# Attention and a maxout layer on one core: fewer turning products, idle products in the opening, bounds of the weights by other products

## The chip, the core and the metric

The kernel runs on one core of a Trainium2 chip. The time is the device time of one execution in microseconds (us), from launch to end, as the median of several runs. The profile is one further execution recorded by the hardware profiler; its span runs from the first to the last instruction of the core.

## What is computed

Queries and keys are normalised per row, an ordinary softmax attention over 448 positions follows for 8 batches of 12 heads, and the heads' outputs, side by side, are the rows of a layer that takes the largest of three products and multiplies it by a fourth matrix:

```python
q, k, v: (8, 12, 448, 64); g_q, g_k: (64,); w1, w2, w3, w_out: (768, 768)

def rmsnorm(x, g):
    rms = np.sqrt(np.mean(x * x, axis=-1, keepdims=True) + 1e-06)
    return x / rms * g
q_n, k_n = (rmsnorm(q, g_q), rmsnorm(k, g_k))
scores = (1.0 / np.sqrt(64)) * np.matmul(q_n, k_n.transpose(0, 1, 3, 2))
scores = scores - np.max(scores, axis=-1, keepdims=True)
attn = np.exp(scores)
attn = attn / (np.sum(attn, axis=-1, keepdims=True) + 1e-09)
attn_out = np.matmul(attn, v)

x = attn_out.transpose(0, 2, 1, 3).reshape(8 * 448, 768)
h = np.maximum(np.maximum(x @ w1, x @ w2), x @ w3)
return h @ w_out
```

Queries, keys, values and gains come as 32-bit floats; the four weight matrices come as 64-bit floats, which the chip loads as pairs of 32-bit words (`raw` tiles) and decodes to 32-bit floats.

## The kernel before

**Groups and beats.** Two heads of a batch make a group `g` (48 of them, six to a batch). The program is one hand-written order: `for g: for i in range(12): beat(g, i)`. A beat puts work on the five engines' queues, and each engine takes its own queue strictly in that order. `later(n, work)` puts work off by `n` beats; `tick()` at a beat's end emits what is due. `thirds(n)` puts about `n` pieces of the maxout layer (three matmuls each) behind the attention's work of a beat, from a queue of batches; a batch of the layer is queued when its six groups are through, so the layer begins with group 6, and after the last group what is left of it runs alone.

**Plain groups.** The first six groups (`g < PLAIN`) work in 32-bit floats throughout: `turn_whole` turns a group's normalised rows (7 blocks of 128 rows by 64) by products with an identity on TensorE, `keep_whole` copies them to SBUF on ScalarE, `scores` multiplies, `row_max` (VectorE) takes the largest of each row, `softmax` (ScalarE) writes `e`, `turn_plain` and `keep_turned` turn it, `add_values` multiplies by v, and `spread_sums` and `keep_sums` spread the reciprocals of the row sums over the 64 columns of each head. From group 6 on, each operand is split in two 16-bit parts, three products stand for one, and turning is done by DMA; those groups are not touched here.

**Opening.** Ahead of the first beat, groups 0 and 1 are loaded, squared (`squares`), summed (`sum_squares`), their inverse root mean squares are taken with a power on GpSimd (`inv_rms`), and group 0 is scaled and turned. `prep_gain` works out the gain's scale with some small operations on VectorE and a power on GpSimd.

**Weights.** 24 blocks of 128 x 768 (18 of w1, w2, w3, in six threes, then 6 of w_out) are loaded, rebased on ScalarE, decoded in three steps on VectorE (`prep_block`), and split in 16-bit parts by `upper` (ScalarE) and `lower` (VectorE), one block every 4 beats and then every 8. The split needs a scale. `bound_in`, once for three blocks, bounds their columns by 18 products of the blocks' upper halves with themselves, into one PSUM tile of 128 x 128, takes each row's largest (`row_largest`), and `largest` takes the largest over partitions: a product that turns the column, a reduction on one partition, and a product that spreads the number over 128 partitions. `clear` sends it to GpSimd for a square root, and `scale` on VectorE copies, inverts and scales it. For w_out each block's largest entry comes from a reduction over its 768 columns in SBUF, and `bound_out` combines them, again with `largest`.

**PSUM.** One pool of three banks (`tag="m"`) serves turned rows, turned weights, bounds and the layer's accumulators `acc`; a bank is given again when it was read.

## Time and profile before

| | |
|---|---|
| median of 3 runs | 1035.94 us |
| the three runs | 1033.67, 1035.94, 1036.47 us |
| profiled execution, its own time | 1033.57 us |
| its span | 1031.8 us |
| mean granted TensorE clock | 0.985 |
| TensorE matmul busy | 988.9 us (96%) |
| VectorE busy | 697.5 us (68%) |
| ScalarE busy | 622.8 us (60%) |
| GpSimd busy | 598.5 us (58%) |

PE is TensorE's matmuls, PEld its weight loads, DVE VectorE, ACT ScalarE, POOL GpSimd, SP the engine whose queue issues most DMAs; SPq and ACTq are the queues' own instructions. `L841` is line 841 of the kernel. A row of a group of instructions names the tile written, `<-`, and the tiles read; in brackets stands how long the engine was idle before, and what ended that. A matmul of 32-bit floats shows as two matmul records. A row of stretches gives, for each engine, its busy time and its number of instructions, then the granted clock of TensorE and the mean share of the DMA engines. In the first 24 us the clock column shows 1.00, though the same products take about twice as long there as later; there their durations tell the clock. As matmuls are pipelined and their ends modelled, a duration of several matmuls holds some 0.2 us of latency.

### The profile page before, as it was taken

To read this page: it belongs to the slowest core of one execution; us is meant where nothing else is said; L and a number is where in the kernel's file an instruction comes from. 1 tells how busy PE (TensorE), PEld (TensorE's weight loads), DVE (VectorE), ACT (ScalarE), POOL (GpSimd) and SP (SyncE) were. 2 spreads that over 40 slices of the span, in tenths; PEclk is the share of its full clock that TensorE was granted. 3 is DMA by queue.
4 is the path that set the end of the run, shared out by engine and by line. 5 is a ranking of instruction groups with operands and counts; after the bars stand their busy time and mean duration, and the time that the engine had idled before them with its cause. 6 is when DMAs were issued, how large, how long until landed. Compare 5 with 4: busy or idle time off the path is not lost.

```text
span 1031.8 us, 17413 instructions
## 1 busy us (share of the span) xinstructions
PE 988.9 (96%) x5988; PEld 530.6 (51%) x5988; DVE 697.5 (68%) x1343; ACT 622.8 (60%) x1419; POOL 598.5 (58%) x652
## 2 busy tenths in 40 slices
PE   5999789898899999999999999999999999999998
PEld 3655444444455555555555555555555555555555
DVE  4898989987676856776667767786777666760120
ACT  3787866667666676666665666666665766651111
POOL 5566676765766666756666576676675766410000
PEclk9999879999999999999999999999999999999999
DMA  8866698997999999999999899999999998861001
GB/s 200 202 178 172 165 204 164 177 166 134 209 173 171 167 182 210 168 172 151 221 171 188 152 216 181 177 169 180 193 168 169 179 201 145 135 104 59 1 1 62
DMA packets 524089, 165.99 MB, mean 161 GB/s; under 512 B 500321, under 2 KB 519777, under 8 KB 524001
## 3 DMA queue, kind: packets, MB, share of 16 engines
q1 hardware_dynamic: 460992, 148.89, 74.8%
q10 hardware_dynamic: 63008, 16.00, 8.7%
q8 instruction: 47, 0.77, 0.3%
q14 instruction: 42, 0.34, 0.1%
HBM read 53.35 MB, written 11.01 MB: 62 GB/s over the span
## 4 chain that ended last, share of the span: by engine, by line
PE 74%; DVE 2%; ACT 1%; DMA 1%; issue 1%; SPq 0%; ACTq 0%
PE acc L841 41%; PE acc L903 15%; PE av L812 8%; PE sc L633 8%; PE sc L640 1%; DVE pp L767 1%; DVE nm L655 1%; DMA pt<-pp 1%; ACT sc L671 0%; DVE w_sb L335 0%; DVE ss L413 0%; DMA out_dram<-osb 0%; SPq L786 0%; ACT w_sb L330 0%; ACT pp L757 0%
## 5 line engine op out<-in xcount | busy, mean ns | idle before, releaser
L841 PE MATMUL acc<-xt,w_sb 128*128 128x448 f16 x2592 | 516.8, 355 | 0.0
L841 PEld LDWEIGHTS <-w_sb 128*128 128x128 f16 x2592 | 252.5, 98 | 245.0 <-issue 16.8
L671 ACT ACTIVATE sc<-sc,nm 128x448 f32<-128x448 f32 x294 | 178.8, 608 | 197.0 <-DVE nm L655 192.5
L655 DVE TENSOR_REDUCE nm<-sc 128x2 f32<-128x896 f32 x192 | 186.3, 970 | 101.5 <-PE sc L640 51.4
L757 ACT ACTIVATE pp<-sc,rs 128x448 f16<-128x448 f32 x294 | 172.8, 633 | 77.9 <-issue 29.2
L767 DVE SCALAR_TENSOR_TENSOR pp<-sc,rs,pp 128x448 f16<-128x448 f32 x294 | 188.0, 675 | 3.3 <-ACT pp L757 3.2
L427 POOL TENSOR_TENSOR ri<-ri,half_neg 128x7 f32<-128x7 f32 x96 | 148.8, 1550 | 8.0
L903 PE MATMUL acc<-w_sb,ht 128*128 128x384 f16 x864 | 148.6, 327 | 0.0
L461 POOL TENSOR_TENSOR kp<-kn,kp 128x448 f16<-128x448 f32 x42 | 44.7, 1065 | 167.6 <-ACT kp L455 154.5
L633 PE MATMUL sc<-kt,qt 128*128 128x448 f16 x504 | 117.6, 356 | 10.4 <-DVE pp L767 7.7
L903 PEld LDWEIGHTS <-ht 128*128 128x128 f16 x864 | 83.8, 99 | 60.2 <-issue 5.8
L633 PEld LDWEIGHTS <-qt 128*128 128x128 f16 x504 | 48.8, 98 | 56.0 <-issue 6.9
L812 PE MATMUL av<-pt,vp 128*64 128x448 f16 x672 | 72.2, 355 | 0.7 <-DMA pt<-pp 0.6
L870 POOL COPY hx<-ht 128x128 f16<-128x128 f16 x48 | 15.3, 318 | 94.3 <-DVE ht L865 94.3
L413 DVE TENSOR_REDUCE ss<-sq 128x7 f32<-128x448 f32 x96 | 57.6, 601 | 11.4 <-ACT sq L404 8.3
L595 POOL TENSOR_TENSOR vp<-vr,vp 128x512 f16<-128x512 f32 x42 | 50.0, 1189 | 22.6 <-ACT vp L589 22.6
L750 DVE TENSOR_SCALAR rs<-sc 128x2 f32<-128x2 f32 (+1 forms) x168 | 26.2, 156 | 50.4 <-ACT sc L671 50.3
L827 DVE SCALAR_TENSOR_TENSOR xt<-av,xt 128x448 f16<-128x448 f32 x42 | 26.2, 623 | 49.0 <-ACT xt L826 49.0
L461 POOL TENSOR_TENSOR qp<-qn,qp 128x448 f16<-128x448 f32 x42 | 46.2, 1100 | 19.2 <-ACT qp L455 16.9
L855 DVE TENSOR_TENSOR m<-acc,m 128x448 f32<-128x448 f32 x48 | 29.6, 617 | 37.7 <-PE acc L841 37.5
L812 PEld LDWEIGHTS <-vp 128*64 128x64 f16 x672 | 35.0, 109 | 35.0 <-issue 15.5
L861 ACT ACTIVATE ht<-acc 128x448 f16<-128x448 f32 x48 | 26.2, 546 | 41.8 <-DVE acc L855 41.8
(130 smaller groups left out, 1181.4 us busy)
## 6 DMA issues: line engine op xcount, KB each, us to landing
raw<-in_moe_w_dram SPq DMA_DIRECT2D x18, 768.0 KB, 4.5
kt<-kt SPq DMA_DIRECT2D x84, 112.0 KB, 2.5
out_dram<-osb SPq DMA_DIRECT2D x24, 384.0 KB, 3.7
vr<-in_v_dram SPq DMA_DIRECT2D x42, 192.0 KB, 4.1
kr<-in_k_dram ACTq DMA_DIRECT2D x34, 224.0 KB, 3.3
qr<-in_q_dram ACTq DMA_DIRECT2D x34, 224.0 KB, 4.6
raw<-in_moe_w_out_dram SPq DMA_DIRECT2D x6, 768.0 KB, 5.0
vs<-vp SPq DMA_DIRECT2D x84, 48.0 KB, 2.1
```

What stands on the lines that cost most here:

```text
L413: nc.vector.tensor_reduce(sums[g % 2][:, KQ[what]], sq, axis=AX, op=ALU.add)
L427: nc.gpsimd.tensor_tensor(out=ri, in0=ri, in1=half_neg[:, at], op=ALU.pow)
L461: nc.gpsimd.tensor_tensor(out=parts[:, :, 1], in0=n, in1=parts[:, :, 0], op=ALU.subtract)
L595: nc.gpsimd.tensor_tensor(out=vp[:, 1], in0=values_of(g).rearrange("p h n d -> p (h n) d"), in1=vp[:, 0], op=ALU.subtract,)
L633: nc.tensor.matmul(sc[:, h, :S], qt[:, 4 * h + c], kt[:, n, keys[h]], start=n == 0, stop=n == 1,)
L655: nc.vector.tensor_reduce(nm[:, :n], sc[:, :n, :S], axis=AX, op=ALU.max, negate=True)
L671: nc.scalar.activation(to, sc[:, h, :S], AF.Exp, bias=nm[:, h:h + 1], accum_out=total,)
L757: nc.scalar.activation(pp[:, h, 0], sc[:, h, :S], AF.Copy, scale=rs[:, h:h + 1])
L767: nc.vector.scalar_tensor_tensor(out=pp[:, h, 1], in0=sc[:, h, :S], scalar=rs[:, h:h + 1], in1=pp[:, h, 0], op0=ALU.mult, op1=ALU.subtract,)
L812: nc.tensor.matmul(av[half, :S], values, pt[:, 7 * h + block, SHIFT[h]:SHIFT[h] + S], start=n == 0, stop=n == len(steps) - 1,)
L841: nc.tensor.matmul(acc[:, :S], wt[:, wp, c], xs[c][:, xp], start=(c == 0 and n == 0), stop=(c == NCT - 1 and n == 2),)
L903: nc.tensor.matmul(acc[:, :HW], lhs, wo_sb[:, f, wp, half * HW:(half + 1) * HW], start=(f == 0 and n == 0), stop=(f == NFT - 1 and n == 2),)
```

## The change

Nothing of groups 6 to 47 or of the maxout layer changes. In short:

1. 36 products of the identity with itself, as 16-bit numbers, stand first on TensorE's queue; nothing reads their tile `idle`.
2. `turn_whole` turns the seventh block by two products of 64 x 64 (one to each half) in place of three wider ones; to match, the order of head 1's rows is rotated, q and k tiles hold 448 columns in place of 512, the keys are written in four interleaved runs by `keep_whole`, and v's first batch is loaded in runs of four rows (three DMAs in place of four).
3. q and k of a plain group are loaded by two DMAs in place of three; group 0's use both SP's and ACT's queue.
4. The opening is reordered: both groups are squared first, group 1's sums stand ahead of group 0's scaling on VectorE, and `prep_gain` comes last.
5. `spread_sums` alternates between the halves.
6. `largest` is gone: one product with a matrix of ones adds the rows' largest over partitions. `clear` comes two beats sooner, GpSimd raises to the power -0.5 and scales with a second instruction, `scale` has no VectorE operation of its own, and the split of three blocks begins three beats sooner.
7. Each block of w_out is bounded by 6 products of its upper halves and a reduction of 128 columns, in place of a reduction of 768; `bound_out` takes the roots on GpSimd.

```diff
+WARM = 36
...
+    idle = ps_m.tile([P, 512], F32, name="idle", tag="m")
+    bits = ident.bitcast(BF16)
+    for _ in range(WARM):
+        nc.tensor.matmul(idle[:, :2 * P], bits[:, :P], bits, start=True, stop=True)
...
         if kind == "out":
-            later(5, lambda: row_largest(o_row[:, ft:ft + 1], f), True)
+            bound_block(ft, f)
...
+        def products():
+            box.append(ps_m.tile([P, 512], F32, name="marks", tag="m"))
+            halves = f.bitcast(BF16).rearrange("p (n t) -> p n t", t=2)
+            for c in range(NCT):
+                part = halves[:, c * P:(c + 1) * P, 1]
+                nc.tensor.matmul(
+                    box[0][:, 0:P], part, part, start=c == 0, stop=c == NCT - 1
+                )
+
+        later(6, products)
+        later(8, lambda: row_largest(o_row[:, ft:ft + 1], box[0][:, 0:P]), True)
...
         def reduce():
             row_largest(most, box[0][:, 0:P])
-            largest(most, clear, (1, 1, 2, 1))
...
+        def spread():
+            box.append(ps_m.tile([P, 512], F32, name="most", tag="m"))
+            nc.tensor.matmul(
+                box[1][:, 0:1], ones_c.broadcast_to([P, P]), most, start=True, stop=True
+            )
...
-            nc.gpsimd.tensor_tensor(out=w_up[:, ft:ft + 1], in0=most, in1=root, op=ALU.pow)
-            later(2, scale)
+            up = w_up[:, ft:ft + 1]
+            nc.gpsimd.tensor_tensor(out=up, in0=most, in1=half_neg[:, 0:1], op=ALU.pow)
+            nc.gpsimd.tensor_scalar(
+                out=up, in0=up, scalar1=2.0 * UP, scalar2=1.0, op0=ALU.mult, op1=ALU.mult
+            )
+            later(3, scale)
 
         def scale():
-            top, up = w_most[:, ft:ft + 1], w_up[:, ft:ft + 1]
-            nc.vector.tensor_copy(top, up)
-            nc.vector.reciprocal(up, top)
-            nc.vector.tensor_scalar(
-                out=up, in0=up, scalar1=2.0 * UP, scalar2=None, op0=ALU.mult
-            )
+            up = w_up[:, ft:ft + 1]
...
-                later(2 + 4 * j, lambda n=n, f=f: upper(n, f), True)
-                later(4 + 4 * j, lambda n=n, f=f: lower(n, f), True)
-
-        later(2, products)
-        later(4, reduce)
+                later(4 * j, lambda n=n, f=f: upper(n, f), True)
+                later(2 + 4 * j, lambda n=n, f=f: lower(n, f), True)
+
+        for at, work in ((2, products), (4, reduce), (5, spread), (7, clear)):
+            later(at, work)
...
-            for h in range(2):
-                on[h].dma_start(out=t[:, h:6:2], in_=rows[:, 4 * h:4 * h + 3])
-            on[1].dma_start(out=t[:, 6], in_=rows[:, 3])
+            on[0].dma_start(out=t[:, 0:7:2], in_=rows[:, 0:4])
+            on[1].dma_start(out=t[:, 1:6:2], in_=rows[:, 4:7])
...
-        for to, of, rows in (
-            (slice(0, LEFT), last, upper),
-            (slice(LEFT + 3 * P, 512), last, lower),
-            (slice(LEFT + 3 * P, 512), n[:, 6], lower),
-        ):
+        for half in HALVES:
             nc.tensor.matmul(
-                turned[:of.shape[1], to], of, ident[:, rows],
-                start=True, stop=True,
+                turned[half, 3 * P:S], n[half, 6], ident[half, half], start=True, stop=True
             )
...
-            t = t.rearrange("p a n -> p (a n)").bitcast(F32)[:, :512]
-            nc.scalar.copy(t, turned)
+            t = t.rearrange("p a n -> p (a n)").bitcast(F32)[:, :S]
+            nc.scalar.copy(
+                t.rearrange("p (u n) -> p n u", u=4),
+                turned[:, :S].rearrange("p (n u) -> p n u", u=4),
+            )
...
-        for h, half in enumerate(HALVES):
-            for c in range(3):
+        for c in range(3):
+            for h, half in enumerate(HALVES):
...
+    for g in range(2):
+        for what in "kq":
+            squares(g, what)
     for what in "kq":
-        squares(0, what)
-    sum_squares(0, "k")
-    inv_rms(0, "k")
-    sum_squares(0, "q")
-    inv_rms(0, "q")
+        sum_squares(0, what)
+        inv_rms(0, what)
     nc.vector.tensor_tensor(out=gain, in0=gains[:, 0], in1=gains[:, 1], op=ALU.mult)
+    sum_squares(1, "k")
     scale_rows(0, "k")
+    sum_squares(1, "q")
     scale_rows(0, "q")
```

On TensorE the opening stood like this before (`kn`, `qn` are the scaled rows of a group, `rows` the turned ones, `sc` the scores, `column` the gain as a column):

```order
L1022 MATMUL column<-ones,gain 64x1 x2
L490 MATMUL rows<-ident,kn 128x128 x3
L501 MATMUL rows<-ident,kn 128x64 x2
L501 MATMUL rows<-ident,kn 64x64
L490 MATMUL rows<-ident,qn 128x128 x3
L501 MATMUL rows<-ident,qn 128x64 x2
L501 MATMUL rows<-ident,qn 64x64
L624 MATMUL sc<-kt,qt 128x448 x4
```

and stands like this now, from the last of the 36 idle products on:

```order
L152 MATMUL idle<-ident 128x256
L523 MATMUL rows<-ident,kn 128x128 x3
L528 MATMUL rows<-ident,kn 64x64 x2
L1050 MATMUL column<-ones,gain 64x1 x2
L523 MATMUL rows<-ident,qn 128x128 x3
L528 MATMUL rows<-ident,qn 64x64 x2
L649 MATMUL sc<-kt,qt 128x448 x4
```

The three products that turned the seventh block became two, and the column came behind the keys.

On VectorE the opening's sums and scalings (`ss` sums of squares, `g_top` the first step of `prep_gain`) stood like this before:

```order
L413 TENSOR_REDUCE ss_88<-sq 128x7 x2
L1016 TENSOR_TENSOR gain<-gains 128x64
L435 TENSOR_TENSOR kn<-kr,ri 128x448
L435 TENSOR_TENSOR qn<-qr,ri 128x448
L172 TENSOR_REDUCE g_top<-gain 128x1
```

and now:

```order
L446 TENSOR_REDUCE ss_125<-sq 128x7 x2
L1041 TENSOR_TENSOR gain<-gains 128x64
L446 TENSOR_REDUCE ss_126<-sq 128x7
L468 TENSOR_TENSOR kn<-kr,ri 128x448
L446 TENSOR_REDUCE ss_126<-sq 128x7
L468 TENSOR_TENSOR qn<-qr,ri 128x448
L158 TENSOR_REDUCE g_top<-gain 128x1
```

Group 1's two sums (`ss_126`) came ahead of group 0's two scalings.

On VectorE, where group 1 ends and group 2 begins, behind the rows' largest of the first bound, stood (`w_sb` decoding steps, `top` the reduction inside `largest`, `w_up` the scale):

```order
L160 TENSOR_REDUCE top<-marks 1x1
L204 SCALAR_TENSOR_TENSOR w_sb<-raw,w_sb 128x768
L209 SCALAR_TENSOR_TENSOR w_sb<-raw,w_sb 128x768
L827 SCALAR_TENSOR_TENSOR xt<-av,v_up,xt 128x448
L655 TENSOR_REDUCE nm<-sc 128x2
L274 TENSOR_SCALAR most<-most 128x1
L200 TENSOR_SCALAR w_sb<-raw 128x768
L204 SCALAR_TENSOR_TENSOR w_sb<-raw,w_sb 128x768
L283 COPY w_most<-w_up 128x1
L284 RECIPROCAL w_up<-w_most 128x1
L285 TENSOR_SCALAR w_up<-w_up 128x1
L209 SCALAR_TENSOR_TENSOR w_sb<-raw,w_sb 128x768
```

and stands now:

```order
L190 SCALAR_TENSOR_TENSOR w_sb<-raw,w_sb 128x768
L284 TENSOR_SCALAR most<-most 128x1
L195 SCALAR_TENSOR_TENSOR w_sb<-raw,w_sb 128x768
L852 SCALAR_TENSOR_TENSOR xt<-av,v_up,xt 128x448
L679 TENSOR_REDUCE nm<-sc 128x2
L186 TENSOR_SCALAR w_sb<-raw 128x768
L190 SCALAR_TENSOR_TENSOR w_sb<-raw,w_sb 128x768
L195 SCALAR_TENSOR_TENSOR w_sb<-raw,w_sb 128x768
```

Four small instructions went, and the one that is left came ahead of a decoding step and a row maximum.

More of the change, by code (lines that the diff above doesn't have):

```diff
@@ L343, in scale @@
                 later(ft + 2, lambda ft=ft: lower(ft), True)
-        largest(most, scale, (1, 2, 2, 2))
+        for at, work in ((2, across), (3, spread), (5, scale)):
+            later(at, work)
     st = {}
@@ L731, in spread_sums @@
                 )
+        for h, half in enumerate(HALVES):
             first = 0 if h else 3 * P
```

90 lines of the change are left out of this document (43 added, 47 removed).

## The prediction

> **What bounds the kernel now.** I read the stretches of the span first, cut where TensorE's idle time ends, then the beginning group by group, then the timeline of the opening. The rows give the stretch, its length, then the busy time of PE, PEld, DVE, ACT and POOL, the clock, DMA share and rate.
>
> ```profile
> 0.00:260.00 260.00, 224.60 (x1389) 125.05 (x1390) 216.80 (x386) 176.07 (x385) 170.56 (x162) 0.95 0.80 176
> 260.00:1031.80 771.80, 764.30 (x4601) 405.53 (x4598) 480.68 (x958) 446.75 (x1035) 427.93 (x491) 1.00 0.85 156
> ```
>
> Behind 260 us PE is busy 764.3 of 771.8 us and every edit lies ahead of it, so what is gained or lost in the first 260 us moves the end one for one: the queue of the layer's work keeps PE filled afterwards. Ahead of it PE sits idle for 260.0 - 224.6 = 35.4 us. The next rows cut that part at the first row maximum of each group (the opening, then groups 1 to 9).
>
> ```profile
> 0.00:16.70 16.70, 6.44 (x28) 4.93 (x30) 5.32 (x22) 5.01 (x9) 5.81 (x13) 1.00 0.78 216
> 31.90:49.70 17.80, 17.80 (x132) 11.11 (x132) 13.94 (x25) 12.73 (x32) 8.97 (x9) 1.00 0.74 188
> 49.70:67.60 17.90, 16.98 (x120) 10.06 (x116) 15.88 (x28) 14.61 (x34) 11.17 (x9) 1.00 0.54 158
> 67.60:86.10 18.50, 16.68 (x116) 10.12 (x116) 17.43 (x28) 15.00 (x34) 11.17 (x9) 1.00 0.71 189
> 86.10:106.50 20.40, 19.14 (x128) 11.58 (x128) 18.07 (x30) 15.15 (x34) 12.50 (x10) 0.92 0.50 146
> 106.50:126.10 19.60, 15.59 (x100) 9.41 (x101) 18.55 (x28) 15.72 (x36) 15.70 (x12) 0.91 0.69 179
> 126.10:150.30 24.20, 18.96 (x95) 8.73 (x93) 21.22 (x46) 16.58 (x36) 17.77 (x15) 0.72 0.96 206
> 150.30:174.70 24.40, 21.91 (x128) 11.09 (x127) 23.46 (x41) 14.10 (x31) 15.84 (x16) 0.93 0.91 182
> 174.70:195.00 20.30, 19.92 (x118) 9.94 (x116) 17.90 (x33) 14.20 (x31) 15.53 (x16) 1.00 0.97 177
> 195.00:216.20 21.20, 18.70 (x112) 9.26 (x109) 20.06 (x36) 12.35 (x29) 13.10 (x14) 1.00 0.97 166
> ```
>
> Three regimes stand there. The opening is a chain: no engine is busy for half of it. Group 1 is PE's (17.80 of 17.80), group 2 nearly so. From group 3 on VectorE is busy for 17.43 of 18.50, 18.55 of 19.60, 23.46 of 24.40: it sets the pace up to group 7, and PE and VectorE take turns in groups 8 and 9. PE's lost clock (0.72 in group 6) follows from its waiting.
>
> **The opening, step by step.** The timeline gives start, duration, engine, line, operation and tile:
>
> ```profile
> 4.48 0.58 ACT L404 ACTIVATE sq<-kr 128x448 f32<-128x448 f32 x1 [2.27 <-DMA kr<-in_k_dram]
> 6.10 1.50 POOL L427 TENSOR_TENSOR ri<-ri,half_neg 128x7 f32<-128x7 f32 x1
> 7.60 0.58 ACT L404 ACTIVATE sq<-qr 128x448 f32<-128x448 f32 x1 [2.54 <-DMA kr<-in_k_dram]
> 8.87 0.62 DVE L435 TENSOR_TENSOR kn<-kr,ri 128x448 f32<-128x448 f32 x1
> 11.17 0.62 DVE L435 TENSOR_TENSOR qn<-qr,ri 128x448 f32<-128x448 f32 x1 [1.68 <-POOL ri L427]
> 12.54 1.36 PE L501 MATMUL rows<-ident,qn 128*128 128x64 f32 x6
> 14.74 3.36 PE L624 MATMUL sc<-kt,qt 64*128 64x448 f32 x8 [0.84 <-ACT qt L517]
> 16.66 1.09 DVE L655 TENSOR_REDUCE nm<-sc 128x2 f32<-128x896 f32 x1 [0.32 <-PE sc L624]
> 20.49 0.90 PE L490 MATMUL rows<-ident,kn 128*128 128x128 f32 x3 [2.39 <-POOL kn L435]
> 86.72 0.52 PE L490 MATMUL rows<-ident,kn 128*128 128x128 f32 x3
> 87.08 0.81 PE L501 MATMUL rows<-ident,kn 128*128 128x64 f32 x6
> 29.74 1.02 PE L624 MATMUL sc<-kt,qt 64*128 64x448 f32 x4
> ```
>
> *Loads and scaling.* The square of group 0's q waited 2.54 us for a load. With two DMAs, one on each queue and directly behind k's, its rows can land between 5.1 (when the square of k is done) and 7.6 as now. The root for q can then follow the first at 7.60 and end at 7.6 + 1.5 and a small scaling, which I put at 0.2, so at 9.3, not some 11.1, so qn's own input gains up to 1.8 us. Against it, group 1's sums now stand ahead of kn and qn on VectorE: two times about kn's 0.62 us, for as many columns, and they wait for group 1's loads, with kn, qn, `prep_gain` and the first row maximum queued behind. I leave kn where it is and let qn gain 1.0 (from -0.5, if those loads are late, to 1.8).
>
> *Turning and scores.* q's turned rows took from 11.8, when qn was done, to 13.90; at full rate that work is 86.72 to 87.89, 1.17 us, and with the seventh block at two small products about 0.8. The first pair of scores at full rate is 1.02 in place of half of 3.36. If the idle products hold the clock this is 1.2 + 0.7 = 1.9 us; if they don't, only the smaller turn counts, about 0.7.
>
> *What is late next.* `prep_gain`'s root now stands on GpSimd behind two more roots for group 1 (1.7 each with their scalings); its own is of one column, and I put it at 0.6, well under the 1.5 of seven: 9.3 + 3.4 + 0.6 = 13.3, and VectorE's last step of it is queued ahead of the first row maximum, so that comes at about 13.8 instead of 16.66: **-2.9 us**. GpSimd then scales group 1's keys at once, where PE waited 2.39 for them at 20.49. That lets the third pair of scores and the products for v come some 6 us earlier, but the weights' and v's loads fill the DMA engines then (0.78 up to 16.7 us at 216 GB/s), so I take no more than **-4.5 us in all at 31.9 us**, between -1 and -6. The 36 idle products cost nothing as long as they are done by 9.5, when kn is: nothing else stands on PE's queue. The strided key copy can cost from 0 to 0.6 us (a second pass over it) on ScalarE, which is busy 15 of 18.5; I take 0.
>
> **Plain groups 1 to 5.** PE's part, from one group:
>
> ```profile
> 97.67 0.87 PE L727 MATMUL spread<-ident,sum 128*64 128x128 f32 x6
> 98.46 0.32 PE L733 MATMUL spread<-ident,sum 64*64 64x64 f32 x2
> 82.10 0.38 PE L157 MATMUL marks<-ident,most 128*1 128x128 f32 x2
> 84.38 0.38 PE L164 MATMUL most<-top,ones 1*128 1x1 f32 x2
> 33.14 0.28 PE L554 MATMUL most<-v_most,ones_c 128*128 128x1 f32 x2
> 36.39 3.23 PE L801 MATMUL av<-pt,vr 112*64 112x448 f32 x16
> ```
>
> The spread is these two rows twice, 2.2 us with the gaps; `av`, whose matmuls alternate between the halves already, takes 3.23 / 16 = 0.20 us for 448 columns where a spread's takes 0.87 / 6 = 0.15 for 128, so alternating lets two run side by side: 2.2 becomes 1.0 to 1.5, saving 0.9. Two turns save 0.45 each (0.81 becomes some 0.35). The bound's two products (0.38 each) become one of 0.28, and one hand-over goes. Together 2.3 us a group. VectorE's part:
>
> ```profile
> L160 DVE TENSOR_REDUCE top<-marks 1x1 f32<-1x128 f32 x7 | 1.9, 276 | 0.6 <-PE marks L157 0.5
> L283 DVE COPY w_most<-w_up 128x1 f32<-128x1 f32 x6 | 0.9, 144 | 0.0
> L284 DVE RECIPROCAL w_up<-w_most 128x1 f32<-128x1 f32 x6 | 1.0, 164 | 0.2
> L285 DVE TENSOR_SCALAR w_up<-w_up 128x1 f32<-128x1 f32 x6 | 0.9, 154 | 0.2
> L172 DVE TENSOR_REDUCE o_row<-w_sb 128x1 f32<-128x768 f32 x6 | 5.6, 938 | 0.0
> L172 DVE TENSOR_REDUCE most<-marks 128x1 f32<-128x128 f32 x6 | 1.7, 280 | 0.8 <-PE marks L265 0.8
> ```
>
> Each bound loses 0.276 + 0.144 + 0.164 + 0.154 = 0.74 us of VectorE, about four of six within these groups: 3.0 us. Group 1 can use PE's saving (VectorE idles 3.9 there), groups 3 to 5 only VectorE's. The earlier split moves some VectorE work forward into group 2. The sum: group 1 -1.8, group 2 -0.3, groups 3 to 5 about -0.5 each, **-3.5 us**, between 0 and -7 (all of PE's five times 2.3 would be 11.5, but VectorE idles only 1.0 to 2.3 in groups 3 to 5).
>
> **Groups 6 to 9.** VectorE loses two bounds (1.5) and six times 0.938 - 0.280 = 0.66 (3.95): 5.4 us. PE gains 36 products more:
>
> ```profile
> 99.77 0.87 PE L543 MATMUL marks<-vr 128*128 128x128 bf16 x12
> ```
>
> at 0.87 / 12 = 0.073 each, 2.6 us, which cost where PE binds (groups 8, 9) and nothing in 6 and 7, where VectorE binds. Their PSUM bank is held for two beats, which could stall an `acc` by 0 to 0.5 us six times; I take 0. GpSimd's added scaling of one column, with 15.5 to 17.8 us busy of 20 to 24, finds room behind the root, and three beats lie between it and the split that reads it. So **-3.5 us**, between 0 and -6.
>
> **The sum.** -4.5 - 3.5 - 3.5 = -11.5. The profiled execution's own time is 1033.57 us (span 1031.8 and 1.8 around it), just under the fastest of the three runs, 1033.67, and 2.4 under their median. 1033.6 - 11.5 = 1022.1; a median lies between 0 and 2.4 above such a run, so I forecast 1023. A measurement here can tell about 0.3%, 3.1 us.
>
> **The rivals.**
> *VectorE and the hand-overs keep the pace.* Where PE is done sooner it only waits longer: the plain groups give 1.5, groups 6 to 9 give 2, the opening 2.9. For it speaks VectorE's 18.55 of 19.60; against it group 1. 1033.6 - 6.4 = 1027, or, with the opening's loads late as well, within 0.3% of no change.
> *The idle products don't hold the clock.* They end ahead of kn and the opening's PE work is thin, so turns and scores run as slow as now: the opening gives 1.5 instead of 4.5, and the time is about 1026.
> *More than the sum.* Group 6 has a clock of 0.72. If an earlier VectorE keeps PE fed, the half-rate stretches go:
>
> ```profile
> 129.71 5.06 PE L801 MATMUL av<-pt,vr 112*64 112x448 f32 x16
> 85.60:89.00 3.40, 2.16 (x17) 1.70 (x17) 3.31 (x7) 3.40 (x10) 1.67 (x2) 1.00 0.83 204
> 89.10:92.40 3.30, 3.30 (x14) 1.84 (x12) 3.30 (x4) 1.44 (x4) 2.01 (x2) 0.50 1.01 234
> ```
>
> `av` took 5.06 there against 3.23; three such places are 5 us: about 1017.
> *The clock turns against it (slower).* PE busy 2.16 of 3.40 us was followed by a stretch at 0.50. With 2.3 us less work in each plain group, PE falls to some 14 of 18.5 and more stretches look like that one. Each costs up to 1.7 us where PE is then late. Seven more than now eat the whole gain, nine more make it slower by over 0.3%; every other stretch of groups 0 to 5 (110 us / 3.4 / 2 = 16) would cost 27 and give 1049. Against it: at full rate there is slack, and one slow stretch refills the next.
>
> The Trainium skill (TensorE: Matmul & The Clock Gate, Parts 1 and 4) says that one idle window of about 3.4 us halves the clock and that transposes on PE do not count as work for it; by that rule the second rival (1026) holds at least, since what is left in the opening is mostly turning, and the last one (1049) gains weight. The trace agrees on the length of the slow stretch, but what preceded it, 2.16 busy of 3.40, is not an idle window.
>
> **How the numbers follow.** Forecast 0.46; VectorE keeps the pace 0.22, of which 0.08 within 0.3%; no clock 0.14; more than the sum 0.10; slower 0.08. Faster is 0.46 + 0.14 + 0.14 + 0.10 = 0.84, same 0.08, slower 0.08. The low end is the third rival with the opening's full 6: 1013. The high end, 1033, leaves out the slower rival and the cases of no change.
>
> **What would show it.** Right: first row maximum near 13.8 us; scores of group 0 about 1.0 us a pair; groups 1 to 5 some 18 us each with VectorE over 17; a spread in one run of about 1.2 us; groups 6 and 7 shorter by 1.3 to 1.8. Wrong: a wait of kn or the first row maximum for group 1's loads, turned rows still at 0.90, a clock below 0.9 in groups 1 to 5, or PE idle at 260 us grown.

## The result, and the profile after

| | before | after |
|---|---|---|
| median | 1036.04 us of 4 runs | 1026.67 us of 4 runs |
| runs | 1033.67 to 1036.47 us | 1023.89 to 1027.25 us |
| profiled execution, its own time | 1033.57 us | 1026.32 us |
| its span | 1031.8 us | 1024.1 us |
| mean granted clock of TensorE | 0.985 | 0.979 |
| VectorE busy in the whole span | 697.5 us | 694.0 us |

The ratio is 0.9909, with a 95% interval of [0.9893, 0.9925]: faster by 9.4 us. The forecast was 1023.0 us.

These are the stretches of the changed kernel, with the columns of the prediction (PE, PEld, DVE, ACT, POOL, clock, DMA share, GB/s): first the two parts of the span, then the opening, group 0 and groups 1 to 9, each cut at a group's first row maximum.

```profile
0.00:260.00 260.00, 227.49 (x1492) 124.85 (x1492) 220.19 (x380) 185.25 (x404) 179.29 (x177) 0.93 0.85 184
260.00:1024.10 764.10, 754.71 (x4534) 401.12 (x4530) 473.77 (x941) 438.86 (x1015) 422.42 (x483) 1.00 0.83 155
...
0.00:18.00 18.00, 10.67 (x60) 7.34 (x62) 5.95 (x22) 5.41 (x9) 9.93 (x17) 0.83 0.76 210
18.00:29.20 11.20, 10.73 (x73) 5.85 (x72) 9.94 (x16) 10.02 (x23) 8.63 (x9) 0.82 1.07 241
29.20:45.60 16.40, 16.40 (x135) 9.94 (x133) 14.31 (x26) 12.93 (x31) 11.48 (x12) 1.00 0.86 220
45.60:63.40 17.80, 16.03 (x125) 9.08 (x121) 17.70 (x25) 16.27 (x36) 12.79 (x12) 1.00 0.57 162
63.40:82.20 18.80, 15.95 (x110) 8.97 (x110) 17.94 (x24) 15.23 (x33) 11.92 (x12) 0.91 0.73 191
82.20:102.50 20.30, 17.20 (x116) 9.60 (x115) 16.26 (x26) 15.08 (x33) 11.17 (x10) 0.83 0.49 143
102.50:121.90 19.40, 15.12 (x96) 8.39 (x96) 19.28 (x25) 15.80 (x35) 17.27 (x12) 0.82 0.74 183
121.90:144.40 22.50, 16.85 (x94) 8.21 (x95) 20.86 (x41) 15.67 (x34) 17.70 (x19) 0.77 0.98 197
144.40:166.60 22.20, 21.53 (x144) 11.59 (x142) 20.77 (x36) 14.81 (x32) 14.35 (x14) 1.00 1.05 210
166.60:186.40 19.80, 19.80 (x121) 10.13 (x120) 16.89 (x33) 13.40 (x30) 14.90 (x16) 1.00 0.97 186
186.40:206.70 20.30, 18.34 (x112) 9.12 (x110) 18.04 (x33) 12.35 (x29) 13.07 (x14) 1.00 0.96 175
```

Ahead of 260 us PE now idles for 260.0 - 227.5 = 32.5 us (35.4 before), and behind it for 764.1 - 754.7 = 9.4 (7.5). The opening is longer by 1.3 us (18.0 against 16.7), but group 0 behind it takes 11.2 instead of 15.2, so group 1 starts 2.7 us sooner. Groups 1 to 5 take 92.7 instead of 94.2, and what they gain lies in groups 1 and 2 alone; groups 3, 4 and 5 run at a clock of 0.91, 0.83 and 0.82, where it was 1.00, 0.92 and 0.91. Groups 6 to 9 take 84.8 instead of 90.1. From the first row maximum of group 10 to the end it is 1024.1 - 206.7 = 817.4 instead of 1031.8 - 216.2 = 815.6, 1.8 us longer, about as much as PE's idle time behind 260 us has grown. Together: 1.3 - 4.0 - 1.5 - 5.3 + 1.8 = -7.7 us, which is the difference of the two spans. The medians lie 9.4 apart, since the profiled execution of before was on the low side of its runs and that of after was not. Each table of stretches is one execution: in the changed kernel and the three tried below that differ from it in a small term only (no idle products, another order of the spread, keys copied in order), groups 1 to 5 take 91.5 to 93.5 us and groups 3 to 7 102.5 to 103.6, so a difference of about 1 us between two such tables is not to be read.

**The opening after.** From the timeline, around the first scores, and the later product for v that group 0 waits for:

```profile
10.33 0.23 DVE L1041 TENSOR_TENSOR gain<-gains 128x64 f32<-128x64 f32 x1 [4.01 <-DMA gains<-in_g_k_dram]
11.75 0.62 DVE L468 TENSOR_TENSOR kn<-kr,ri 128x448 f32<-128x448 f32 x1
16.08 3.36 PE L649 MATMUL sc<-kt,qt 64*128 64x448 f32 x8 [0.79 <-ACT qt L546]
17.99 1.09 DVE L679 TENSOR_REDUCE nm<-sc 128x2 f32<-128x896 f32 x1 [0.65 <-PE sc L649]
27.26 0.73 PE L572 MATMUL marks<-vr 112*128 112x128 bf16 x10 [0.47 <-DMA vr<-in_v_dram]
```

Group 0's keys are scaled at 11.75, where they were at 8.87: ahead of them on VectorE stand the product of the gains, whose load it waited 4.01 us for, and the sum of group 1's keys, whose load ended ScalarE's idle time at 10.61. The first alone would have let them start at 10.56 (10.33 + 0.23); the sum makes it 11.75. The turned rows still take 0.90 and the first scores 3.36 us. The stretches of the clock in the opening show why:

```profile
5.00:8.40 3.40, 2.23 (x20) 1.76 (x18) 0.69 (x2) 0.58 (x1) 2.98 (x4) 1.00 0.32 77
8.40:11.90 3.50, 0.00 (x0) 0.00 (x0) 0.91 (x3) 1.15 (x2) 0.43 (x1) 0.99 0.98 313
11.90:15.30 3.40, 2.86 (x18) 1.88 (x18) 2.66 (x11) 0.98 (x2) 3.13 (x4) 0.50 0.99 330
```

The idle products end at 7.2 us, TensorE then does nothing until 12.4, and the clock is at half from 11.9 on. What the idle products bought was spent in that pause: in the trace the first of them start 0.21 us apart and the last 0.11 us, so the clock had been raised. The Trainium skill (TensorE: Matmul & The Clock Gate, Part 1) says that the clock falls to half after one window of about 3.4 us without work; the row of 0.00 us from 8.40 to 11.90 and the 0.50 behind it agree.

**TensorE's part in a plain group**, from the timeline of group 3 (the rows turned, then the spread):

```profile
72.59 0.55 PE L523 MATMUL rows<-ident,qn 128*128 128x128 f32 x3
73.06 0.33 PE L528 MATMUL rows<-ident,qn 64*64 64x64 f32 x4
74.46 0.88 PE L751 MATMUL spread<-ident,sum 128*64 128x128 f32 x12
75.27 0.33 PE L758 MATMUL spread<-ident,sum 64*64 64x64 f32 x4
```

A turn takes 0.80 us, forecast 0.8; the spread 1.14 us, forecast 1.0 to 1.5. Both sizes held.

### The profile page after: what moved, and what is told of

It is laid out like the page before. It is cut to its first block, busy times and chain, and to the rows that moved or that the text cites. A ratio compares the mean times of both kernels' runs of the same rounds, so it can differ in the third digit from the quotient of the medians.

```text
span 1024.1 us, 17454 instructions
## 1 busy us (share of the span) xinstructions
PE 982.2 (96%) x6022; PEld 526.0 (51%) x6022; DVE 694.0 (68%) x1320; ACT 624.1 (61%) x1419; POOL 601.7 (59%) x659
## 4 chain that ended last, share of the span: by engine, by line
PE 74%; DVE 2%; ACT 1%; DMA 1%; issue 1%; SPq 0%; DVEq 0%; ACTq 0%
PE acc L866 41%; PE acc L928 15%; PE av L837 8%; PE sc L657 8%; PE sc L664 1%; DVE nm L679 1%; DVE pp L792 1%; DMA pt<-pp 1%; ACT sc L695 0%; DVE w_sb L359 0%; DMA out_dram<-osb 0%; DVE ss L446 0%; ACT w_sb L354 0%; DVE v_rows L158 0%; DVE m L880 0%
## 5 line engine op out<-in xcount | busy, mean ns | idle before, releaser
L866 PEld LDWEIGHTS <-w_sb 128*128 128x128 f16 x2592 | 251.5, 98 | 241.7 <-issue 12.4
L928 PEld LDWEIGHTS <-ht 128*128 128x128 f16 x864 | 83.5, 98 | 59.5 <-issue 4.7
L895 POOL COPY hx<-ht 128x128 f16<-128x128 f16 x48 | 15.4, 321 | 94.2 <-DVE ht L890 94.2
L456 POOL TENSOR_SCALAR ri<-ss 128x7 f32<-128x7 f32 x54 | 17.5, 325 | 58.8 <-DVE ss L446 57.9
```

The source lines that it names most:

```text
L866: nc.tensor.matmul(acc[:, :S], wt[:, wp, c], xs[c][:, xp], start=(c == 0 and n == 0), stop=(c == NCT - 1 and n == 2),)
L928: nc.tensor.matmul(acc[:, :HW], lhs, wo_sb[:, f, wp, half * HW:(half + 1) * HW], start=(f == 0 and n == 0), stop=(f == NFT - 1 and n == 2),)
```

## The experiments

Ratios are to the kernel before, with 95% intervals; where nothing else is said, a diff is against the changed kernel, whose own ratio is 0.9909 [0.9893, 0.9925].

### What are the bounds worth, and where?

One kernel is the changed one with the bounds of before (`largest` back, the reduction over 768 columns back, the split where it was):

```diff
-            bound_block(ft, f)
+            later(5, lambda: row_largest(o_row[:, ft:ft + 1], f), True)
...
+            largest(most, clear, (1, 1, 2, 1))
...
-                later(4 * j, lambda n=n, f=f: upper(n, f), True)
-                later(2 + 4 * j, lambda n=n, f=f: lower(n, f), True)
+                later(2 + 4 * j, lambda n=n, f=f: upper(n, f), True)
+                later(4 + 4 * j, lambda n=n, f=f: lower(n, f), True)
```

> The changed kernel with the bounds of the weights as they were (three products and reductions for the first layer, reductions of 768 columns for the second, the split three beats later). Theory: the bounds' VectorE work and hand-overs pay in groups 6 to 9, whose 84.8 us go back to about 89 to 90, and little in groups 1 to 5; the time is 1031 to 1033. Rival: the gain of groups 6 to 9 comes from the other edits (an earlier start, another phase of the clock); then the time stays at 1025 to 1028.

The other is the kernel before with the new bounds alone (parts 6 and 7 of the change); against before, its diff is

```diff
-            later(5, lambda: row_largest(o_row[:, ft:ft + 1], f), True)
+            bound_block(ft, f)
...
-            largest(most, clear, (1, 1, 2, 1))
...
+        for at, work in ((2, products), (4, reduce), (5, spread), (7, clear)):
+            later(at, work)
```

> The kernel before with the new bounds alone. Theory: it gains what the run with the old bounds loses, 4 to 6 us, so 1030 to 1032, all of it in groups 6 to 9. Rival: alone they gain nothing, 1035 to 1037, and the opening and the plain groups carry the change.

Measured: 0.9953 [0.9941, 0.9965] with the old bounds, 0.9952 [0.9933, 0.9971] with the new bounds alone. So the bounds are worth 0.44% to 0.48%, some 4.5 to 5 us, and everything else in the change about as much; the two add up to the whole. Both theories held in this: groups 6 to 9 go back to 89.3 us, and alone the bounds gain there; the times, 1030.0 and 1029.6 us, lie just under the two forecasts (the kernel before took 1034.5 in the same set of runs). The stretches of groups 1 to 5 and of groups 6 to 9, of the kernel with old bounds:

```profile
29.60:120.80 91.20, 80.28 (x584) 45.45 (x583) 86.42 (x134) 75.16 (x165) 60.99 (x49) 0.94 0.66 178
120.80:210.10 89.30, 78.12 (x441) 37.73 (x440) 82.50 (x153) 56.66 (x125) 62.12 (x58) 0.91 0.98 185
```

The kernel before with new bounds alone takes 95.5 us (32.5 to 128.0) and 83.5 us (128.0 to 211.5) for the same groups. So in groups 6 to 9 the bounds take 4.5 us off (89.3 to 84.8) or 6.6 (90.1 to 83.5). In groups 1 to 5 they add time, 1.5 us (91.2 to 92.7) or 1.3 (94.2 to 95.5), and the other edits take 3.0 us off (94.2 to 91.2). The two figures of added time agree, but each is hardly more than two such tables can differ by.

### Do the idle products do anything?

```diff
-    idle = ps_m.tile([P, 512], F32, name="idle", tag="m")
-    bits = ident.bitcast(BF16)
-    for _ in range(WARM):
-        nc.tensor.matmul(idle[:, :2 * P], bits[:, :P], bits, start=True, stop=True)
```

> The changed kernel without the 36 idle products. Theory: they end at 7.2 us, the clock is back at half from 11.9, and the first turned rows come at 12.4 and take 0.90 for three as before; so they buy nothing, and without them the time stays within 1.5 us of the changed kernel (1025 to 1028), with the first row maximum at 18.0 as now. Rival: they shorten the opening; then the time rises by 2 us or more, to 1029.

Measured: 0.9905 [0.9893, 0.9917], the first row maximum at 18.0 us as with them. They buy nothing in this order that the times show. In the profiles group 0 takes 12.0 us without them and 11.2 with them, but in the two kernels with mixed splits below 11.1 without and 12.0 with.

### Is the first row maximum late because the weights' loads are early?

In the changed kernel the three weight blocks are asked for at 4.43 us (7.51 before), so their bytes go through the DMA engines together with the gains and group 1's rows. One kernel moves the three loads behind group 2's:

```diff
     load_q(1)
-    for _ in range(3):
-        load_raw()
...
     load_q(2)
+    for _ in range(3):
+        load_raw()
```

> The changed kernel with the first three loads of weights issued behind the loads of group 2 instead of ahead of them. Theory: with fewer DMAs ahead of it SP issues these 768 KB loads at 4.4 us instead of 7.5, they share the DMA engines with the gains and group 1, the gains land at 10.2 instead of 8.0, and VectorE, with the first keys' scaling queued behind, waits 4.0 us for them. Held back, the gains land by 8, the keys are scaled by 9, the first row maximum comes 2 to 3 us sooner, at 15 to 16, and the time falls to 1023 to 1025. Rival: the gains are late by their own slow packets; then nothing moves, 1025 to 1028.

Measured: 0.9945 [0.9934, 0.9957], 1028.9 us, slower than theory and rival had it. Its timeline, the first row maximum and the later products for v's first half:

```profile
16.08 1.09 DVE L679 TENSOR_REDUCE nm<-sc 128x2 f32<-128x896 f32 x1 [0.66 <-PE sc L649]
...
25.63 1.23 PE L572 MATMUL marks<-vr 112*128 112x128 bf16 x10 [1.21 <-DMA vr<-in_v_dram]
```

The first half of the theory held: the keys (9.84) and the first row maximum came 1.9 us sooner. The second fell: v, queued behind the weights on SP, came later, TensorE waited for it, here 1.21 us and 2.80 us just before, and group 1 began at 32.6 instead of 29.2.

So the next kernel puts the blocks one at a time between the other loads:

```diff
     load_q(1)
-    for _ in range(3):
-        load_raw()
...
     load_q(2)
+    load_raw()
...
+        if g == 0 and i in (1, 3):
+            load_raw()
```

> The changed kernel with the first weight block's load behind the loads of group 2, the second behind v's first and group 3's, the third behind v's second. Theory: the opening is limited by what the DMA engines have to move by the time it is needed; with all three blocks held back the gains landed at 8.5 instead of 10.2 and the first row maximum came at 16.1, but v's first load landed at 25 instead of 22 and group 0 took 16.5 us instead of 11.2. One block at a time, v lands by 19, group 0 takes 11 us or less, group 1 begins at 27 instead of 29.2, and the time is 0.2 to 0.3% under the changed kernel's (a ratio of 0.988 to 0.989 to the kernel before). Rival: a later wait in the plain groups swallows it (ratio 0.990 to 0.992).

and its companion has idle products until the keys are there:

```diff
-WARM = 36
+WARM = 54
```

(with the loads as in the one before).

> The same with 54 idle products instead of 36. Theory: they now end at about 9.5 to 10.5 us, where the first turned keys begin, so the clock is at full rate there; turned rows take 0.5 instead of 0.9 for three and the first two pairs of scores 1.8 instead of 3.4, the first row maximum comes at about 15, and group 1 begins some 1 us sooner than without. Rival: the clock falls back in the thin work behind them and nothing moves, as with 36 or none.

Measured: 0.9941 [0.9927, 0.9955] and 0.9958 [0.9946, 0.9971]; both slower than the changed kernel and than either forecast for the first. With single blocks the first row maximum stands at 15.3 us, but the DMA engines now have a hole (the stretch from 8.4 us), because group 2's loads wait for a buffer that the scaling of the keys frees, and v is no sooner:

```profile
8.40:12.00 3.60, 1.88 (x14) 1.37 (x14) 3.15 (x11) 1.66 (x4) 2.55 (x4) 0.81 0.21 47
```

A share of 0.21 stands there where the changed kernel has 0.98. The later products for v begin at 27.16, where they did at 27.26, and group 1 starts at 29.8, not at 27 as the theory had it. With more idle products the opening has these rows (the first scores and `prep_gain`'s last step):

```profile
13.08 1.77 PE L649 MATMUL sc<-kt,qt 64*128 64x448 f32 x8 [0.79 <-ACT qt L546]
...
14.35 0.92 DVE L1029 TENSOR_SCALAR gain<-gain,even 128x64 f32<-128x64 f32 x1 [1.68 <-POOL even L1028]
```

The clock holds (1.00 from 11.90 to 15.30, where the changed kernel has 0.50), and the scores take 1.77 instead of 3.36 us. The row maximum is at 15.18, hardly sooner than without them: ahead of it on VectorE stands `prep_gain`'s last step, which waits 1.68 us for GpSimd. A clock that is held buys nothing when the scores are not what the row maximum waits for. Group 1 starts at 31.8, later than without the added products.

### Does the first row maximum matter at all?

The last test of the opening moves no load. Group 0's keys and queries are scaled and turned ahead of all that waits for the gains or for group 1, and `prep_gain` comes behind the first row maximum:

```diff
+    for what in "kq":
+        scale_rows(0, what)
     nc.vector.tensor_tensor(out=gain, in0=gains[:, 0], in1=gains[:, 1], op=ALU.mult)
-    sum_squares(1, "k")
-    scale_rows(0, "k")
-    sum_squares(1, "q")
-    scale_rows(0, "q")
+    for what in "kq":
+        sum_squares(1, what)
...
-    prep_gain()
...
     row_max(0, 0)
+    prep_gain()
```

> The changed kernel with group 0's keys and queries scaled and turned ahead of everything that waits for the gains or for group 1's rows, and prep_gain behind the first row maximum; no load is issued in another order. Both theories: keys scaled at about 7.0 us instead of 11.75, the first row maximum at 13 to 15 us instead of 18.0. Theory: the opening ends when the DMA engines have moved v and the next groups' rows, so group 1 still starts at 28 to 29.5 us and the ratio to the kernel before stays at 0.989 to 0.991. Rival, the chain of the first scores sets it: group 1 starts at 25 to 26 us and the ratio is 0.986 to 0.988.

Measured: 0.9928 [0.9915, 0.994]. From its timeline:

```profile
6.92 0.63 DVE L468 TENSOR_TENSOR kn<-kr,ri 128x448 f32<-128x448 f32 x1 [0.75 <-POOL ri L460]
...
14.90 1.09 DVE L679 TENSOR_REDUCE nm<-sc 128x2 f32<-128x896 f32 x1 [2.60 <-PE sc L649]
...
27.91 0.73 PE L572 MATMUL marks<-vr 112*128 112x128 bf16 x10 [1.02 <-DMA vr<-in_v_dram]
```

The keys are scaled 4.8 us sooner and the first row maximum comes 3.1 us sooner, and group 1 starts at 29.9, 0.4 us past the theory's range and no sooner than in the changed kernel. The ratio lies above both forecasts. The rival, that the chain of the first scores sets the opening, falls: what ends it is the load of v. In this kernel TensorE waits 1.02 us for v's last rows, and group 1 starts 2.0 us behind that product's start, as it does in the changed kernel (27.26 and 29.2).

### Why do the new bounds cost time in groups 1 to 5?

The three extra beats by which the splits come sooner are taken back:

```diff
-            later(3, scale)
+            later(4, scale)
...
-                later(4 * j, lambda n=n, f=f: upper(n, f), True)
-                later(2 + 4 * j, lambda n=n, f=f: lower(n, f), True)
+                later(2 + 4 * j, lambda n=n, f=f: upper(n, f), True)
+                later(4 + 4 * j, lambda n=n, f=f: lower(n, f), True)
```

> The changed kernel with the split of the first layer's blocks three beats later, where it stood before; the new bounds stay. Theory: in groups 1 to 5 the new bounds take VectorE work away and yet those groups are 1.2 to 1.5 us longer with them than with the old ones, because the earlier split puts a lower part (1.0 us on VectorE) ahead of the row maximum that opens a group, for which ScalarE and then PE wait. Then groups 1 to 5 fall from 92.7 to 90 or 91 and groups 6 to 9 stay at 85: a ratio of 0.988 to 0.9895. Rival: the place of the split doesn't matter, 92 to 93, ratio 0.9905 to 0.9915.

Measured: 0.989 [0.9873, 0.9907]; groups 1 to 5 take 90.1 us (92.7), as the theory had it, but groups 6 to 9 take 87.2 (84.8), where it had 85, and the time is not to be told from the changed kernel's. At the start of group 3 the changed kernel has these rows (VectorE's lower half of a split, the row maximum, and the next scores, which wait for ScalarE's `e`):

```profile
62.45 1.00 DVE L302 SCALAR_TENSOR_TENSOR w_sb<-w_sb,w_up 128x768 f16<-128x768 f32 x1
...
63.38 1.08 DVE L679 TENSOR_REDUCE nm<-sc 128x2 f32<-128x896 f32 x1
...
65.88 1.32 PE L649 MATMUL sc<-kt,qt 64*128 64x448 f32 x4 [2.96 <-ACT e L695]
```

and the one with the later splits these:

```profile
63.17 1.07 DVE L679 TENSOR_REDUCE nm<-sc 128x2 f32<-128x896 f32 x1
...
65.68 1.02 PE L649 MATMUL sc<-kt,qt 64*128 64x448 f32 x4 [1.75 <-ACT e L695]
65.81 1.01 DVE L302 SCALAR_TENSOR_TENSOR w_sb<-w_sb,w_up 128x768 f16<-128x768 f32 x1
```

Sooner by three beats, the lower half stands ahead of the row maximum that ScalarE and then TensorE wait for; three beats later it stands behind it. TensorE's wait goes from 2.96 to 1.75 us, and its next scores run at full rate (1.02) instead of in part at half (1.32).

It seemed to follow that each part could have its own placing: late splits for the first four bounds, early for the last two. The first kernel does that, the second also leaves out the idle products:

```diff
+            off = (3, 3, 3, 3, 2, 1)[ft]
...
-                later(4 * j, lambda n=n, f=f: upper(n, f), True)
-                later(2 + 4 * j, lambda n=n, f=f: lower(n, f), True)
+                later(off + 4 * j, lambda n=n, f=f: upper(n, f), True)
+                later(off + 2 + 4 * j, lambda n=n, f=f: lower(n, f), True)
```

> The changed kernel with the splits of the first four bounds three beats later, as in the kernel before, that of the fifth two and of the sixth one beat later. Theory: each part of the beginning pays for its own placing, so groups 1 to 5 take 90 to 91 us (as with all splits late: 90.1) and groups 6 to 9 take 85 to 86 (as with all splits early: 84.8); the ratio to the kernel before is 0.986 to 0.989. Rival: groups 6 to 9 are longer with late splits because the chain of bounds arrives later as a whole; then they stay at 87 and the ratio is that of all splits late, 0.989 to 0.990.

```diff
-WARM = 36
+WARM = 0
```

> The same with no idle products. Theory: they buy nothing, so the ratio is within 0.2% of that of the run with the mixed splits, and the first row maximum stands at 17.5 to 18.5 us. Rival: at these splits a group 0 that is 0.8 us shorter with the idle products (11.2 against 12.0) comes through, and the ratio is 0.1 to 0.2% higher without them.

Measured: 0.9912 [0.9894, 0.9929] and 0.993 [0.9911, 0.995]. The theory fell. Groups 1 to 5 take 87.6 us, less than it said, and groups 6 to 9 take 88.5, more than with all splits late; without the idle products they take 89.0 and 88.7. Here are groups 3 to 7 as one stretch, first of the kernel before, then of the changed one, of all splits late and of mixed splits:

```profile
67.60:174.70 107.10, 92.29 (x563) 50.92 (x564) 98.74 (x169) 76.55 (x167) 72.99 (x61) 0.89 0.77 181
```

```profile
63.40:166.60 103.20, 86.64 (x557) 46.76 (x558) 95.11 (x147) 76.59 (x166) 72.42 (x64) 0.87 0.81 185
```

```profile
63.20:166.80 103.60, 86.68 (x566) 46.63 (x567) 96.51 (x147) 77.00 (x167) 70.59 (x64) 0.88 0.80 187
```

```profile
62.30:165.90 103.60, 84.07 (x573) 45.81 (x574) 97.88 (x148) 78.11 (x168) 71.76 (x65) 0.92 0.80 189
```

From group 3 to group 7 the time is 103.2 to 103.6 us in the last three, wherever the splits stand; the mixed kernel without idle products has 104.9 (VectorE busy 97.0). VectorE's column (98.74, 95.11, 96.51, 97.88) points to why: in the last three it is busy for 92 to 94% of the time, so moving its work from one group to the next moves the boundary between them and not the end. What goes with the 3.9 us by which the stretch is shorter is work taken from VectorE (98.74 to 95.11, 3.6 us) or idle time taken from it. The new bounds alone do the first, and the same groups take 103.8 us (VectorE 95.6, idle 8.2); the other edits alone do the second, 104.8 us (VectorE 100.2, idle 4.6 instead of 8.4). Alone they give 3.3 and 2.3 us, together 3.9. The Trainium skill (Perfetto Trace Analysis, Identifying the Most-Contended Engine and Optimization Strategy) says to optimize the engine of the highest occupancy first, and that the most-contended engine can change over time; in these five groups that engine is VectorE, at 92% (95.11 of 103.2). As to the idle products, 0.9912 with and 0.993 without, where the earlier pair was 0.9909 with and 0.9905 without: no difference that these intervals can tell.

### Smaller terms: the spread's order and the strided copy of the keys

```diff
-        for c in range(3):
-            for h, half in enumerate(HALVES):
+        for h, half in enumerate(HALVES):
+            for c in range(3):
                 first = LEFT * h + c * P
```

> The changed kernel with only the order of the spread's products undone (one half's three, then the other's). Theory: the spread takes 2.0 to 2.2 us a group again instead of 1.15, PE has slack in groups 3 to 5 where the row maximum comes late, so of the five times 1.0 us only 1 to 2 us show in groups 1 to 5 (93.7 to 94.7 against 92.7), and the ratio to the kernel before is 0.991 to 0.993. Rival: nothing shows, since PE waits for the scalar engine's e anyway: 92.7 and 0.991 or below.

Measured: 0.992 [0.9891, 0.9949]. The spread in that kernel, from its timeline:

```profile
75.81 1.14 PE L751 MATMUL spread<-ident,sum 128*64 128x128 f32 x12
76.88 0.33 PE L758 MATMUL spread<-ident,sum 64*64 64x64 f32 x4
```

Theory and rival both assumed 2.0 us or more here, and it takes 76.88 + 0.33 - 75.81 = 1.40. So of the 1.0 us saved in a spread, 0.77 come from the small products, which now stand last instead of between the halves, and only 0.26 from taking the halves in turn. The time shows no difference: groups 1 to 5 take 93.5 us (92.7), and the interval holds both the theory's ratios and the rival's.

```diff
-            nc.scalar.copy(
-                t.rearrange("p (u n) -> p n u", u=4),
-                turned[:, :S].rearrange("p (n u) -> p n u", u=4),
-            )
+            nc.scalar.copy(t, turned[:, :S])
```

The keys then stand in another order than v's rows.

> The changed kernel with the keys of a plain group copied in the order in which they stand, so its six first groups weight the wrong rows of v; the work is otherwise the same. Theory: the copy in four interleaved runs takes 0.92 us instead of 0.58, six times on ScalarE, which isn't the limit; back in order it takes 0.55 and the time stays within 0.1% of the changed kernel's (ratio 0.990 to 0.992). Rival: the copy stands between turned keys and scores, and 6 times 0.37 us come off the end (ratio about 0.989).

Measured: 0.9904 [0.989, 0.9917]. All copies of the keys in this run, with the shortest, the mean and the longest in ns (915, 934 and 952 in the changed kernel):

```profile
L539 ACT COPY kt<-rows x6: 527/535/539, 13.5 to 86.3; 128x448 f32<-128x448 f32 x6
```

The strided copy costs 934 - 535 = 399 ns more each time, in a place where ScalarE has room; the forecast took 0 of the possible 0 to 0.6 for the time. No difference can be measured, but the rival's 0.989 lies at the lower end of the interval and is not excluded.

## Why the prediction was right or wrong

**The total** lay within the range, 3.7 us above the forecast. Against the sum for the span (-11.5) stand -7.7: the opening gave 1.8 us too little, the part behind group 10, forecast at nothing, took 1.8 us back, and groups 1 to 9 gave 6.8 of the 7.0 forecast. Within these 6.8 one part gave 2.0 us too little and the other 1.8 too much. Three of the four signs of being wrong came: the keys waited behind group 1's sums, the turned rows stayed at 0.90, and the clock fell below 0.9 in groups 4 and 5. Of the signs of being right the spread (1.14 us) and groups 6 and 7 (1.7 and 2.2 us shorter, forecast 1.3 to 1.8) came; the first row maximum and the first scores did not.

**The opening: wrong in its chain, half right in its sum.** The step that failed is "I leave kn where it is and let qn gain 1.0". The prediction saw that group 1's sums, and the loads that they wait for, would stand ahead of the keys, and priced it at nothing. With the product of the gains, which stands there too, they cost 2.9 us (11.75 instead of 8.87), of which 1.2 (10.56 to 11.75) are the sum's. It did not see that the weights' loads, asked for 3 us sooner, would share the DMA engines with the gains: these landed at 10.23 us instead of 7.95, and came at 8.46 when the weights were put later, with the keys at 9.84. From that followed the second rival's event: the idle products ended 5.2 us ahead of the keys, and the clock did not hold. Nor would earlier keys have been enough: with keys first, scaled at 6.92, the rows were turned at full rate (0.55) and the scores still took 3.36. So the first row maximum was 1.3 us later instead of 2.9 sooner. But that number was not what the opening hung on. Brought forward by 3.1 us it moved nothing, and group 0 became 4.0 us shorter with a later one.

What ends the opening, in the changed order, is v's last load: it landed at 27.12 us, TensorE's products for these rows begin at 27.26, and in all twelve kernels with that opening or a variant of it they begin 0.13 or 0.14 us behind the landing. Landing and start of group 1 go together (27.1 and 29.2 in the changed kernel, 27.0 and 29.8 with single blocks, 27.8 and 29.9 with keys first, 28.6 and 31.8 with more idle products, 30.6 and 32.6 with the weights later). In the kernels that share the changed opening (old bounds, later and mixed splits, the spread's order) they vary from 27.1 and 29.2 to 28.2 and 30.2, so the changed kernel's gain of 2.7 us at this point stands at the upper end of 1.7 to 2.7. For the order of before it is not shown: v landed at 28.88 there, and TensorE came to its products at 28.89 without an idle time (the row below); with the new bounds alone, which keep that opening, v landed at 28.16, the products began 1.6 us later, and group 1 started at 32.5.

```profile
28.89 0.91 PE L543 MATMUL marks<-vr 112*128 112x128 bf16 x12
```

Why v landed 1.76 us sooner no run took apart, but SP's queue shows a part of it. These rows are GpSimd's scaling of group 1's keys and the first load of group 3, before and then after:

```profile
19.50 0.93 POOL L435 TENSOR_TENSOR kn<-kr,ri 128x448 f32<-128x448 f32 x1
20.46 0.92 SPq L358 DMA_DIRECT2D kr<-in_k_dram  x2
...
16.35 0.94 POOL L468 TENSOR_TENSOR kn<-kr,ri 128x448 f32<-128x448 f32 x1
18.19 0.39 SPq L382 DMA_DIRECT2D kr<-in_k_dram  x1
```

Before, SP waited 2.1 us for that scaling, which frees the buffer, and v's second load stood behind on its queue; now the scaling is done when SP comes to the load. v's last DMA was issued at 21.95 instead of 25.09. So the prediction's "GpSimd then scales group 1's keys at once" was right, and it worked through a load. The third pair of scores and the first products for v came 1.9 and 2.4 us sooner, not 6 (20.61 and 23.89, before 22.48 and 26.27). What the fewer DMAs (groups 1 to 3 and v's first batch in 18 instead of 26) add to that is open. The sentence "the weights' and v's loads fill the DMA engines then" had this bound in it, as a caution instead of a term.

**Plain groups 1 to 5: -1.5 instead of -3.5.** TensorE's terms were right in size (turn 0.80, spread 1.14), though the spread's reason was not: 0.77 of its 1.0 us come from the small products put last, not from alternating. Without the new bounds these groups give 3.0 us. Groups 1 and 2 gave 1.5 of the 2.1 forecast for them, groups 3 to 5 nothing of 1.5 (the terms add up to 3.6, not 3.5). The step that failed is VectorE's part, "about four of six within these groups: 3.0 us". The removed operations are gone, yet VectorE was busy longer in these groups, 85.5 against 83.9 (the five rows of each kernel). The first step of the decoding, as a group of instructions over groups 1 to 5, after and then before, shows what filled it:

```profile
L186 DVE TENSOR_SCALAR w_sb<-raw 128x768 uint32<-128x768 uint32 x15 | 10.9, 729 | 0.0
```

```profile
L200 DVE TENSOR_SCALAR w_sb<-raw 128x768 uint32<-128x768 uint32 x15 | 8.8, 589 | 0.0
```

The same fifteen operations take 2.1 us more, and the second step of the decoding, by the same view, 2.3 more (16.8 instead of 14.5): 4.4 us, which eat the 3.0. Where it hurt within these groups is the earlier split, which stands ahead of the row maximum (2.6 us, by the run with later splits, which loses 2.4 of them again in groups 6 to 9). "The earlier split moves some VectorE work forward into group 2" was given no cost. The last rival's picture came true in small: PE fell to 15.1 to 17.2 us busy a group, and groups 3 to 5 had 17 us at half rate instead of 7; groups 3 to 5 took 58.5 us together, as before.

**Groups 6 to 9: -5.3 instead of -3.5.** The mechanism was right. VectorE's 5.4 us less were forecast to show in part; they showed nearly in full, and part of it is what groups 3 to 5 had not gained: over groups 3 to 7 as one, VectorE has 3.6 us less and the time is 3.9 us shorter. What TensorE's 36 added products (2.6 us) cost, and their PSUM bank, was not measured apart; in group 8 TensorE is now busy for all of the 19.80 us. That groups 1 to 5 and 6 to 9 were forecast apart, as if each kept its own gain, was the mistake; the sum over both came right because what one part lacked the other had.

**Behind group 10: +1.8 instead of 0.** Nothing there is changed, and yet this part takes 814.9 us (new bounds alone) to 819.4 (keys first) in the fourteen kernels of this document, so the 1.8 us do not stand clear of how this part varies from kernel to kernel. Groups 10 to 13, with nearly the same instructions, take 78.0 us with the keys in order, 78.9 before, 80.2 in the changed kernel and 81.8 with keys first, at clocks of 1.00, 0.96, 0.98 and 0.96: the clock does not put them in order. What makes one longer than another was not settled.

**The rivals.** The first, in which VectorE and the hand-overs keep the pace, has the median (1027 against 1026.67) and two of its three terms (plain groups 1.5 and 1.5, opening 2.9 and 2.7) closer than the forecast has them; the gain in groups 6 to 9 was larger than its 2, and the part behind group 10 took the rest back, so its total is in part luck. The second's event came (no clock in the opening), but the 3 us that it put on it are not shown: with the clock held group 1 started no sooner. The changed kernel does not stand clear of the version without idle products or of the one with later splits; no version tried is shown to beat it.

## What to carry to other kernels

Before pricing a chain in an opening, look for what its last wait is on: here, in the changed order, it was a load at 27 us, and the row maximum that the sum was made for could move by 3 us (18.0 to 14.9) without moving the end. Where one engine is over 90% busy across several stages, forecast them as one: work moved between them moves only their boundary, what is taken from that engine, work or idle time, is what showed here. An instruction put earlier on a strict queue is a cost to whatever it now stands ahead of.

## What the runs showed of the hardware that was not expected

- One pause is enough to lose a raised clock: 36 products up to 7.2 us, a stretch from 8.40 to 11.90 with none, and half rate from 11.9 to 22. A stretch need not be empty for that: the kernel with keys first had TensorE busy for 1.03 us between 8.40 and 11.90 (the row below) and ran at 0.53 from there to 15.30, where 2.23 of 3.40 (the changed kernel, from 5.00 to 8.40) was still followed by 0.99. So here more than the wholly idle window that the Trainium skill (TensorE: Matmul & The Clock Gate, Part 1) names was followed by half rate:

```profile
8.40:11.90 3.50, 1.03 (x13) 0.70 (x11) 1.70 (x4) 1.41 (x4) 1.01 (x2) 1.00 0.99 319
```

- VectorE's and GpSimd's wide steps take longer when they meet. These rows of the changed kernel's timeline are the first decoding step on VectorE and a square on GpSimd, in two places:

```profile
46.60 0.55 DVE L186 TENSOR_SCALAR w_sb<-raw 128x768 uint32<-128x768 uint32 x1
46.63 1.31 POOL L439 TENSOR_TENSOR sq<-qr 128x448 f32<-128x448 f32 x1
...
64.21 0.93 POOL L439 TENSOR_TENSOR sq<-qr 128x448 f32<-128x448 f32 x1
64.38 1.17 DVE L186 TENSOR_SCALAR w_sb<-raw 128x768 uint32<-128x768 uint32 x1
```

Where VectorE's step begins first it takes 0.55 us and the square 1.31; where the square is under way it takes 0.93 and the step 1.17. Of the fifteen such steps in groups 1 to 5, the four that took 1.12 to 1.29 us all began while a multiplication of 128 x 448 on GpSimd had 0.7 to 0.9 us to go; the others, which met none or its last 0.2 us, took 0.54 to 0.59. Before, two of the fifteen met one and took 1.01 and 0.68, the others 0.54 to 0.56. The Trainium skill (GPSIMD Engine Reference, Specifications) says that GpSimd's way to SBUF is shared with VectorE and that it is in contention with VectorE's instructions in a two-port mode or with two inputs from SBUF. The rows agree in that the later of the two takes longer by somewhat less than what is left of the other (0.38 us of 0.52 and 0.62 of 0.76); no run here moved them apart, so that this is the cause was not shown.
- A copy on ScalarE that writes each next 32-bit number 112 places on, in runs of four, took 0.93 us, one of the same 128 x 448 in order 0.54.
